# Windowed attention and a mixture of experts: expert 0's second weights and the zero blocks issued later, nine value slots, and gate logits in pieces of 64 keys by 32 columns

## The chip, the cores and the metric

The kernel runs on one core of a Trainium2 chip. The metric is the device time of one execution in microseconds (us). Matmuls run on TensorE (PE; the loading of their weights is shown apart, as PEld), elementwise work on VectorE (DVE), ScalarE (ACT) and GpSimd (POOL). SyncE (SP) issues most of the DMA transfers, in the order in which they are written.

## The reference

Attention over a window of 64 positions, then a layer of 8 experts of which each row takes its best two.

```python
scores = scale * np.matmul(q, k.transpose(0, 1, 3, 2))      # 8 batches, 8 heads, 576 positions, 64 dims
mask = (rel >= 0) & (rel < window)                           # window = 64
attn = softmax(np.where(mask, scores, -1e9))
x = np.matmul(attn, v) ...                                   # rows of 512: N = 4608
noisy_logits = x @ w_gate + np.log1p(np.exp(x @ w_noise)) * noise
top2 = the two largest of 8 per row, with softmax weights
for e in range(E):                                           # E = 8, w1 512 x 1024, w2 1024 x 512
    h = np.maximum(x[mask] @ w1[e], 0.0)
    out[mask] += top2_w[mask, k, None] * (h @ w2[e])
```

## The kernel before

The attention is done in 36 units. A unit j is a block of 64 positions (i = j // 4) of a pair of batches (bp = j % 4), with all 8 heads. The loop over j, near the end of the program, is a software pipeline written out by hand: in iteration j PE does the scores of unit j (`scores`), the product with the values of unit j-2 (`pv`), the transposes of the probabilities of unit j-1 (`transp`) and the gate logits of the values of unit j (`logits`). ACT copies the scores out of PSUM (`soft_a`, tile t), takes the exponential (`soft_b`, tile p), scales the output of unit j-3 (`norm_b`, tile x) and copies the logits out (`logits_copy`). DVE puts in the previous block's scores (`soft_max`), takes the maximum, masks the transposed probabilities (`apply_mask`, tile pt) and does most of the routing. POOL subtracts the maximum (line 342) and builds one-hot rows for the routing (line 592). Each engine runs its instructions in the order written.

The gate logits are linear in the attention output. So the gate's weights are multiplied with the values first: each value slot VW holds, beside four groups of values, a fifth group of 16 columns with the logits of each key, and `pv` averages them over the window together with the values. `logits` makes them on PE from a transposed copy of the values (vT, tile vt): for each of four pairs q of heads one matmul with 128 keys as weight columns (two batches of 64) and 64 moving columns, of which each key needs 32. `logits_copy` therefore takes for each half of the partitions the half of the columns that belongs to it, in two instructions.

Loads go through SP: q and k three units ahead, values (`load_v`, line 131) behind `pv`, vT (`load_vt`, line 137) behind `logits`. A value slot is a half of a tile VW[bp], for an even or an odd block: the load for unit j+2, issued behind `pv(j-2)`, overwrites values that this very `pv` reads. vT has two buffers, and the load for j+2 overwrites the one that `logits(j)` reads.

Two more kinds of transfer stand in that loop. In units 32 to 35 the second weights of expert 0 are loaded (`load_w2`, line 219; 8 pieces of 256 KB). They go to the tile ws, and `split_w2` (lines 243 and 235) cuts them into two parts while the first layer of expert 0 runs. From unit ZFROM = 36 on, `zero_out` (line 199) writes blocks of 128 rows of zeros to the output, three a unit, 38 blocks in all; the rest of them is spread over the layers of expert 0. The experts' results are added to the output by indirect transfers from POOL (line 966), which need the zeros of their rows first.

Units 36 to 38 only finish the pipeline. Between their pieces, and before that from unit 32 on the transposes for it (line 734), the first layer of expert 0 (`up(0, 0)`) begins. What follows is the work on the experts, 16 pairs of layers, in which PE runs almost without a gap.

Of the kernel before, what the change touches and what calls it, by code (L numbers as in the profile page):

```python
# [8 lines left out]
F32 = mybir.dt.float32  # L9
# [4 lines left out]
AF = mybir.ActivationFunctionType  # L14
# [6 lines left out]
NP = B // 2  # L21
NT = NP * NB
# [21 lines left out]
SLOTS = 5  # L44
WARM = 4

ZFROM = 36
PACED = 12
HOLD = 4
RATE = ((16, 8), (99, 7))  # L50
# [38 lines left out]
def tile_kernel(ctx, tc, qT, kT, vx, vT, wgx, noise, w1, w2, out):  # L89
    nc = tc.nc  # L90
# [14 lines left out]
    acon = at.enter_context(tc.tile_pool(name="acon", bufs=1))  # L105
    ld = at.enter_context(tc.tile_pool(name="ld", bufs=2))
    wk = at.enter_context(tc.tile_pool(name="wk", bufs=2))
# [1 line left out]

    KW = acon.tile([128, NP, 2, H, 64], F32)  # L110

    VW = [acon.tile([128, 2, 5, 2, 4, 17], F32, name=f"vw{j}") for j in range(NP)]
    QC, VT = {}, {}

    def load_q(j):
# [12 lines left out]

    def load_v(j):
        i, bp = divmod(j, NP)  # L130
        nc.sync.dma_start(VW[bp][:, i % 2, 0:4], vx[bp, i])


    def load_vt(j):
        i, bp = divmod(j, NP)
        VT[j] = ld.tile([128, 4, 128], F32, name="vt", bufs=2)
        nc.sync.dma_start(VT[j], vT[bp, i])

    for j in range(2):
# [33 lines left out]
    nc.vector.tensor_scalar(mcur, mprev, -1.0, 1.0, op0=OP.mult, op1=OP.add)  # L173

    maskT = acon.tile([128, 2, 2, 64], F32)
    other = acon.tile([128, 2, 64], F32)
    o3 = ones.rearrange("p (u r) -> p u r", u=2)
    nc.gpsimd.affine_select(maskT[:, 0], o3, pattern=[[0, 2], [1, 64]], base=0, channel_multiplier=-1,
                            compare_op=OP.is_ge, fill=0.0)
# [2 lines left out]
    nc.vector.tensor_copy(maskT[64:128, 0], other[64:128])  # L182
    nc.vector.tensor_scalar(maskT[:, 1], maskT[:, 0], -1.0, 1.0, op0=OP.mult, op1=OP.add)
    for v in VW:
        nc.gpsimd.memset(v[:, :, 4], 0.0)


    noise_sb = consts.tile([128, NT, E], F32)
# [28 lines left out]
    def load_w2(e, ks=slice(0, KF)):  # L217
        if e < E:
            nc.sync.dma_start(w2s[:, ks], w2[e][:, ks])
# [57 lines left out]
        return lag([(w2s[:, f], W2["h"][:, f], W2["l"][:, f]) for f in (0, 4, 1, 5, 2, 6, 3, 7)])  # L277


    VG = idle[:, 0:256].rearrange("p (n c) -> p n c", n=1)  # L280

    def logits(j):
        p = VG[:, 0]
        x = VT.pop(j)
        for u in range(2):
            for g in range(2):
                q = u * 2 + g
                nc.tensor.matmul(p[:, q * 64:q * 64 + 64], lhsT=x[:, q, :], rhs=wgx_sb[:, g], start=True, stop=True)

    def logits_copy(j):  # L290
        i, bp = divmod(j, NP)
        for a in range(2):
            h = slice(a * 64, a * 64 + 64)
            nc.scalar.activation(VW[bp][h, i % 2, 4, :, :, 0:16].rearrange("p u (g x) e -> p (u g) x e", x=2),
                                 VG[h, 0].rearrange("p (k a x e) -> p k a x e", a=2, x=2, e=16)[:, :, a], AF.Copy)

    ST, T, P, TP, PT, XT = {}, {}, {}, {}, {}, {}

# [67 lines left out]
    def pv(j):  # L366
        i, bp = divmod(j, NP)
        o = aps.tile([128, 2, 512], F32, name="ps_o", bufs=2)
        OT[j] = o
        PO[j] = o[:, :, 0:340].rearrange("p a (k d) -> p a k d", d=85)  # L370
        pt, v = PT.pop(j), VW[bp]
        for g in range(2):
            for x in range(2):
                for w in range(2 if i else 1):
                    for a in range(2):
                        for u in range(2):
                            pa = slice(a * 64, a * 64 + 64)
                            nc.tensor.matmul(PO[j][u * 64:u * 64 + 64, a, g * 2 + x, :],  # L378
                                             lhsT=pt[pa, w, u * 2 + g, x * 64:x * 64 + 64],
                                             rhs=v[pa, (i + w) % 2, :, u, g * 2 + x, :],  # L380
                                             start=(w == 0), stop=(w == 1 or not i))
        if j + NP < NT:
            load_v(j + NP)
# [64 lines left out]
    for k in (1, 2, 4, 8, 16, 32):  # L448
        n = min(k, NT - k)
# [654 lines left out]
    for j in range(NT + 3):  # L1104
        if j == TURN:
            for q, f in enumerate(turn(0, 0)):
                aux.setdefault(j + q // 2, []).append(f)

        if 0 < j < PACED:
            load_k(j + 3)  # L1110
        on(store, j - 4)
        blanks(j)
        if j < 2:
            load_v(j + 2)
        if NT - 4 <= j < NT:
            load_w2(0, slice((j - NT + 4) * 2, (j - NT + 4) * 2 + 1))
        on(norm_a, j - 3)
        drain(rate(0))
        on(scores, j)
        if j < NT - 3:  # L1120
            load_q(j + 3)
        if W1G // 2 - 4 <= j < W1G // 2 + 4:
            k = j - W1G // 2 + 4
            load_w1(0, slice(k // 2, k // 2 + 1), slice(k % 2 * F // 2, (k % 2 + 1) * F // 2))
        if 2 < j < 3 + len(REST):
            REST[j - 3]()
        on(soft_a, j)
        on(soft_b, j - 1)
        ahead(2)
        drain(rate(1))  # L1130
        on(pv, j - 2)
        on(place_slots, j - 2)
        if PACED <= j < NT - 3:
            load_k(j + 3)
        if NT - 4 <= j < NT:
            load_w2(0, slice((j - NT + 4) * 2 + 1, (j - NT + 5) * 2))
        blanks(j)
        on(norm_b, j - 3, 0)
        on(soft_max, j)
        on(soft_max2, j)  # L1140
        if placed:
            add_slots(placed.pop())
        drain_slots(1)
        if j < NP:
            warm(WARM)
        on(transp, j - 1)
        ahead(2)
        on(logits, j)
        if j < NT - 2:
            load_vt(j + 2)  # L1150
        blanks(j)
        on(norm_b, j - 3, 1)
        on(apply_mask, j - 1)
        drain(rate(2))
        on(logits_copy, j)
        ahead(2)
        on(gate, j - 3)
        drain(rate(3))
        drain_slots(2 if j >= DENSE else 1 + j % 2)
        for f in aux.get(j, ()):  # L1160
            f()
        drain(rate(4))
# [18 lines left out]
    for n, (e, c) in enumerate(work):  # L1181
        nxt = work[n + 1] if n + 1 < len(work) else None
        last = c == len(chunks(e)) - 1
        side, parts = [], []
        if n == 2:
            load_counts()
        if n == 0:
            halves = split_w2()
            side += halves[:5]
            parts.append((0.0, 1.0, [lambda: drain_slots(1)] * 9))  # L1190
            parts.append((0.0, 0.35, [zero_out] * 7))

            def catch_up():
                while (0, 1, 2) not in XG:
                    drain(1)
                    drain_slots(1)
        elif n == 1:
            pending.append(count())
            parts.append((0.0, 0.9, [lambda: (drain(1), drain_slots(1))] * 18))
            parts.append((0.0, 0.9, [zero_out] * 8))  # L1200
            side += [settle, lambda: drain_slots(10 ** 6), lambda: [x() for x in first_list(2)]]
        elif c == 0:
            parts.append((0.55, 1.0, split_w2()))
        if nxt and n:
            rows_of = gather(*nxt)
            if n < 2:
                side += [lambda: None] * 2 + rows_of
            else:
                parts.append((0.0, 0.65, rows_of))
        if last and nxt:  # L1210
            nextw = split_w1(e == 0)
            parts += ([(0.55, 0.75, nextw[0]), (0.8, 1.0, nextw[1])] if e else
                      [(a, b, nextw[q]) for q, a, b in ((0, 0.02, 0.12), (1, 0.14, 0.3), (2, 0.33, 0.5), (4, 0.34, 0.5),
                                                       (3, 0.55, 0.75), (5, 0.56, 0.75), (6, 0.8, 1.0))])
        parts.append((0.92 if n == 1 else 0.0, 1.0, side))
        spread(up(e, c) if n else up00, 52 if e else KF * KD - (0 if n else len(taken)), *parts)
        side = turn(*nxt) if nxt else []
        total = KF * len(tiles(e, c)) + (4 if e else 0) - (KF - 1 if chunks(e)[c] % 128 else 0)
        free = 12.5 / total
        if e == 0:  # L1220
            parts = [((0.66, 0.98) if n == 0 else (0.5, 0.97) if n == 1 else (0.02, 0.7)) + (side,)]
            if last:
                parts.append((0.7, 0.98, nextw[7]))
        else:
            if c == 0:
                load_w1(e + 1)
            parts = [(free, 0.86, side)]
            if last and nxt:
                parts.append((free, 0.9, nextw[2] + nextw[3]))
        if n == 1:  # L1230
            load_w1(1)
            parts.append((0.0, 0.6, list(other_lists())))
            parts.append((0.0, 0.4, [zero_out] * len(blank)))
        if n == 0:
            parts.append((0.0, 0.16, halves[5:]))
            parts.append((0.1, 0.96, [lambda: drain(2)] * 24))
            parts.append((0.0, 0.9, [zero_out] * 13))
            parts.append((0.0, 0.6, [lambda: drain_slots(1)] * 6))
            parts.append((0.64, 0.65, [catch_up]))
        spread(down(e, c), total, *parts)  # L1240
        if last:
            load_w2(e + 1)
# [118 lines left out]
```

## Time and profile before

| what | value |
|---|---|
| median of 3 runs | 998.04 us (997.68 to 999.22) |
| the profiled execution | 997.35 us |
| its span, first to last instruction | 995.3 us |
| mean granted TensorE clock | 0.997 of full speed |
| PE busy | 956.3 us (96% of the span) |
| DVE / ACT / POOL busy | 689.9 / 525.9 / 320.1 us |

The share of PE is a mean over a long part in which it is full and a first part of about 195 us in which it is not. Times below are counted from the first instruction of the profiled execution.

### The profile page before, as it was taken

The page shows a single profiled execution, that of the slowest core. Times are in us where ns is not written, and L with a number is a line of the kernel's source. Part 1 is how long each engine was busy: PE and PEld are TensorE (multiplying, and loading weights), DVE is VectorE, ACT ScalarE, POOL GpSimd, SP SyncE. Part 2 cuts the span into 40 slices and gives each one's busy share as a digit, 9 for nine tenths or more (in the row PEclk, how much of TensorE's full clock was granted, in tenths as well). Part 3 has the DMA queues.
Part 4 walks back from the last instruction along what each step waited for, and adds up shares of the span by engine and source line. Part 5 has one row for each costly group of instructions (what it writes and reads, how often), then busy time and mean ns, then how long its engine had stood idle before and what let it go on. Part 6 is the DMA issues. An engine that isn't in the chain of part 4 may idle for free. (4 is left out here: it accounts for less than half of the span.)

```text
span 995.3 us, 21900 instructions
## 1 busy us (share of the span) xinstructions
PE 956.3 (96%) x8408; PEld 858.2 (86%) x8408; DVE 689.9 (69%) x1728; ACT 525.9 (53%) x1346; POOL 320.1 (32%) x442
## 2 busy tenths in 40 slices
PE   8788888999999999999999999999999999999996
PEld 8777787888879888989898989898989898989895
DVE  5688898763786777767766786668666867686730
ACT  4888877522455545544554455445544554455531
POOL 5346546122322414040414141413131323241303
PEclk9999999999999999999999999999999999999999
DMA  9989997894649456854584458454945494647304
GB/s 326 365 270 314 287 294 273 271 263 119 153 89 267 81 130 132 252 73 120 116 265 70 125 115 267 60 134 87 283 63 143 73 266 89 149 93 206 48 1 56
DMA packets 107810, 168.93 MB, mean 170 GB/s; under 512 B 13424, under 2 KB 57712, under 8 KB 105904
## 3 DMA queue, kind: packets, MB, share of 16 engines
q1 hardware_dynamic: 90544, 126.96, 41.7%
q0 software_dynamic: 17152, 40.48, 21.9%
q8 instruction: 68, 1.11, 0.5%
q14 instruction: 46, 0.38, 0.1%
HBM read 110.08 MB, written 57.32 MB: 168 GB/s over the span
## 5 line engine op out<-in xcount | busy, mean ns | idle before, releaser
L966 POOL DMA_INDIRECT out_dram<-xg,los x70 | 111.9, 1598 | 427.5 <-ACT xh L774 124.3
L900 ACT ACTIVATE hb<-tq 128x288 fp32r<-128x288 f32 (+1 forms) x168 | 76.9, 458 | 143.9 <-DVE tq L919 143.7
L1038 PE MATMUL ps_d<-w2h,hb 128*128 128x512 f32 x392 | 152.9, 390 | 0.0
L1039 PE MATMUL ps_d<-w2l,hb 128*128 128x512 f32 x392 | 152.8, 390 | 0.0
L1040 PE MATMUL ps_d<-w2h,hb 128*128 128x512 f32 x392 | 152.7, 390 | 0.0
L919 DVE TENSOR_TENSOR tq<-ps_z,tq 128x288 f32<-128x288 f32 (+1 forms) x168 | 79.2, 472 | 89.0 <-PE ps_z L890 88.5
L888 PE MATMUL ps_z<-xh,WH 128*128 128x288 f32 (+1 forms) x448 | 137.5, 307 | 0.9
L889 PE MATMUL ps_z<-xl,WH 128*128 128x288 f32 (+1 forms) x448 | 135.2, 302 | 0.0
L890 PE MATMUL ps_z<-xh,WL 128*128 128x288 f32 (+1 forms) x448 | 135.2, 302 | 0.0
L904 DVE SCALAR_TENSOR_TENSOR hb<-tq,hb 128x320 fp32r<-128x320 f32 (+2 forms) x168 | 75.6, 451 | 37.5 <-ACT hb L900 35.2
L888 PEld LDWEIGHTS ps_z<-xh,WH 128*128 128x128 f32 x448 | 84.0, 188 | 5.5 <-DVE tq L919 3.7
L1040 PEld LDWEIGHTS ps_d<-w2h,hb 128*128 128x128 f32 x392 | 73.6, 188 | 15.6
L1038 PEld LDWEIGHTS ps_d<-w2h,hb 128*128 128x128 f32 x392 | 73.6, 188 | 14.0
L1039 PEld LDWEIGHTS ps_d<-w2l,hb 128*128 128x128 f32 x392 | 73.6, 188 | 13.8
L889 PEld LDWEIGHTS ps_z<-xl,WH 128*128 128x128 f32 x448 | 84.1, 188 | 1.1
L890 PEld LDWEIGHTS ps_z<-xh,WL 128*128 128x128 f32 x448 | 84.1, 188 | 0.0
L698 POOL DMA_INDIRECT xg<-xrows,lxs x70 | 69.0, 986 | 23.2 <-issue 22.6
L782 ACT ACTIVATE xh<-tq 128x512 fp32r<-128x512 f32 (+1 forms) x70 | 42.7, 610 | 61.9 <-DVE tq L778 60.5
L235 DVE TENSOR_TENSOR WL<-ws,WH 128x512 fp32r<-128x512 f32 x112 | 67.2, 615 | 6.6 <-ACT WH L243 6.5
L399 ACT ACTIVATE x<-ps_o,r 128x80 f32<-128x80 f32 x288 | 67.0, 350 | 7.5 <-DVE r L389 7.2
L378 PE MATMUL ps_o<-vw,pt 64*64 64x85 f32 x2176 | 49.9, 235 | 12.7 <-issue 8.2
L342 POOL TENSOR_TENSOR t<-t,mx 128x512 f32<-128x512 f32 x36 | 38.8, 1078 | 70.8 <-DVE mx L341 49.2
(242 smaller groups left out, 2347.0 us busy)
## 6 DMA issues: line engine op xcount, KB each, us to landing
ws<-in_w_dram SPq DMA_DIRECT2D x14, 2048.0 KB, 11.5
xs<-xg SPq DMA_DIRECT2D x63, 256.0 KB, 3.4
vw<-in_vx_dram SPq DMA_DIRECT2D x36, 272.0 KB, 4.5
out_dram<-zero SPq DMA_DIRECT2D x38, 256.0 KB, 4.6
qc<-in_qT_dram SPq DMA_DIRECT2D x36, 256.0 KB, 4.8
KW<-in_kT_dram SPq DMA_DIRECT2D x36, 256.0 KB, 4.9
vt<-in_vT_dram SPq DMA_DIRECT2D x36, 256.0 KB, 4.6
xrows<-x SPq DMA_DIRECT2D x36, 256.0 KB, 4.9
```

Source lines behind the costliest of these rows:

```text
L235: eng.tensor_tensor(l, x, h.bitcast(F32), op=OP.subtract)
L698: nc.gpsimd.indirect_dma_start(out=XG[e, c, q][:m], out_offset=None, in_=X[:DUMP + seen.get((e, c), NT) * 128], in_offset=bass.IndirectOff ...
L888: nc.tensor.matmul(p[:, :n], lhsT=WH[:, a, k, w], rhs=xh[:, b, k, :n], start=first and k == 0, stop=False, **free)
L889: nc.tensor.matmul(p[:, :n], lhsT=WH[:, a, k, w], rhs=xl[:, b, k, :n], start=False, stop=False, **free)
L890: nc.tensor.matmul(p[:, :n], lhsT=WL[:, a, k, w], rhs=xh[:, b, k, :n], start=False, stop=(k == 1), **free)
L900: nc.scalar.activation(hh[:, f, a:b], src, AF.Relu)
L904: nc.vector.scalar_tensor_tensor(hl[:, f, a:m], src[:, :m - a], 0.0, hh[:, f, a:m].bitcast(F32), op0=OP.max, op1=OP.subtract)
L919: nc.vector.tensor_tensor(t, a[:, :n], t, op=OP.add)
L966: s = nc.gpsimd.indirect_dma_start(out=out[:(2 + seen.get((e, c), NT)) * 128], out_offset=bass.IndirectOffsetOnAxis(ap=LT[e, c][1][q][:m], ...
L1038: nc.tensor.matmul(p, lhsT=h, rhs=w2h[:, f, :], **a)
L1039: nc.tensor.matmul(p, lhsT=h, rhs=w2l[:, f, :], start=False, stop=False)
L1040: nc.tensor.matmul(p, lhsT=l, rhs=w2h[:, f, :], **b)
```

## The change

Four edits. The value slots become nine tiles, used in turn by j, and vT gets a third buffer. The logits are made with 64 keys and 32 columns in a matmul, so that each half of the partitions gets only its own columns; one copy then takes them all. The second weights of expert 0 are loaded in units 34 to 37. No zero block is written in units 36 to 38 any more, and the first layer of expert 0 issues 16 instead of 7. A mask's scratch tile moves to another pool, to make room.

```diff
-ZFROM = 36
+ZFROM = NT + 3
...
-    VW = [acon.tile([128, 2, 5, 2, 4, 17], F32, name=f"vw{j}") for j in range(NP)]
+    VW = [acon.tile([128, 5, 2, 4, 17], F32, name=f"vw{j}") for j in range(2 * NP + 1)]
...
-        nc.sync.dma_start(VW[bp][:, i % 2, 0:4], vx[bp, i])
+        nc.sync.dma_start(VW[j % len(VW)][:, 0:4], vx[bp, i])
...
-        VT[j] = ld.tile([128, 4, 128], F32, name="vt", bufs=2)
+        VT[j] = ld.tile([128, 4, 128], F32, name="vt", bufs=3)
...
-    other = acon.tile([128, 2, 64], F32)
+    other = wk.tile([128, 8, 64], F32, name="t")[:, 0:2]
...
-        nc.gpsimd.memset(v[:, :, 4], 0.0)
+        nc.gpsimd.memset(v[:, 4], 0.0)
...
-                nc.tensor.matmul(p[:, q * 64:q * 64 + 64], lhsT=x[:, q, :], rhs=wgx_sb[:, g], start=True, stop=True)
+                for a in range(2):
+                    h = slice(a * 64, a * 64 + 64)
+                    nc.tensor.matmul(p[h, q * 32:q * 32 + 32], lhsT=x[:, q, h], rhs=wgx_sb[:, g, a * 32:a * 32 + 32],
+                                     start=True, stop=True)
...
-        for a in range(2):
-            h = slice(a * 64, a * 64 + 64)
-            nc.scalar.activation(VW[bp][h, i % 2, 4, :, :, 0:16].rearrange("p u (g x) e -> p (u g) x e", x=2),
-                                 VG[h, 0].rearrange("p (k a x e) -> p k a x e", a=2, x=2, e=16)[:, :, a], AF.Copy)
+        nc.scalar.activation(VW[j % len(VW)][:, 4, :, :, 0:16].rearrange("p u (g x) e -> p (u g) x e", x=2),
+                             VG[:, 0].rearrange("p (k x e) -> p k x e", x=2, e=16), AF.Copy)
...
-        pt, v = PT.pop(j), VW[bp]
+        pt, v = PT.pop(j), [VW[(j - w * NP) % len(VW)] for w in range(2)]
...
-        if NT - 4 <= j < NT:
-            load_w2(0, slice((j - NT + 4) * 2, (j - NT + 4) * 2 + 1))
+        if NT - 2 <= j < NT + 2:
+            load_w2(0, slice((j - NT + 2) * 2, (j - NT + 2) * 2 + 1))
...
-            parts.append((0.0, 0.35, [zero_out] * 7))
+            parts.append((0.05, 0.75, [zero_out] * 16))
```

On PE, a unit of the middle of the attention (scores, values, transposes, logits, and the next unit's scores), before:

```order
L318 MATMUL ps_s<-KW,qc 64x128 x16
L378 MATMUL ps_o<-vw_91,pt 64x85 x32
L354 MATMUL ps_t<-ident,p 128x128 x4
L288 MATMUL ps_g<-wgx_sb,vt 128x64 x4
L318 MATMUL ps_s<-KW,qc 64x128 x16
```

The end of that unit and the start of the next one, now:

```order
L379 MATMUL ps_o<-vw_98,pt 64x85 x4
L355 MATMUL ps_t<-ident,p 128x128 x4
L290 MATMUL ps_g<-wgx_sb,vt 64x32 x8
L319 MATMUL ps_s<-KW,qc 64x128 x16
L379 MATMUL ps_o<-vw_94,pt 64x85 x4
L379 MATMUL ps_o<-vw_90,pt 64x85 x4
```

The four logits matmuls have become eight of a smaller shape in the same place; the product with the values reads two tiles in turn.

On SP, a unit's loads in the middle of the attention with the semaphores that each waits for (DMAHW: an earlier transfer of SP's own; PE, Activation: an engine), before:

```order
L402 DMA xrows<-x 128x512 [waits DMAHW0_49,Activation_49]
L118 DMA qc<-in_qT_dram 128x512 [waits DMAHW1_49,PE_49]
L131 DMA vw_92<-in_vx_dram 128x544 [waits DMAHW2_49,PE_49]
L122 DMA KW<-in_kT_dram 128x512 [waits DMAHW3_49]
L137 DMA vt<-in_vT_dram 128x512 [waits DMAHW4_49,PE_49]
```

And now:

```order
L403 DMA xrows<-x 128x512 [waits DMAHW0_49,Activation_49]
L118 DMA qc<-in_qT_dram 128x512 [waits DMAHW1_49,PE_49]
L131 DMA vw_93<-in_vx_dram 128x544 [waits DMAHW2_49]
L122 DMA KW<-in_kT_dram 128x512 [waits DMAHW3_49]
L137 DMA vt<-in_vT_dram 128x512 [waits DMAHW4_49]
```

The loads of values and vT no longer wait for PE. On SP at the end of the attention (L402 and L403 are the stores of the attention's rows, L579 and L580 of the gate weights, L199 the zero blocks), before:

```order
L219 DMA ws<-in_w_dram 128x512 x2
L579 DMA xrows<-xc 128x6x16
L402 DMA xrows<-x 128x512
L199 DMA out_dram<-zero 256x1x256 x3
L402 DMA xrows<-x 128x512
L199 DMA out_dram<-zero 256x1x256 x3
L402 DMA xrows<-x 128x512
L199 DMA out_dram<-zero 256x1x256 x3
L402 DMA xrows<-x 128x512
L199 DMA out_dram<-zero 256x1x256 x19
L579 DMA xrows<-xc 128x9x16
```

And now:

```order
L580 DMA xrows<-xc 128x6x16
L403 DMA xrows<-x 128x512
L219 DMA ws<-in_w_dram 128x512 x2
L403 DMA xrows<-x 128x512
L219 DMA ws<-in_w_dram 128x512 x2
L403 DMA xrows<-x 128x512 x2
L199 DMA out_dram<-zero 256x1x256 x28
L580 DMA xrows<-xc 128x9x16
```

The last two pairs of w2 pieces stand where six zero blocks stood, and all zero blocks up to the last gate weights stand in one row.

## Rows read from the trace of the kernel before

**Rows 1.** Stretches, columns: PE, PEld, DVE, ACT, POOL busy (x), clock, DMA share, GB/s.

```profile
20.28:48.53 28.25, 22.38 (x586) 20.66 (x585) 17.94 (x28) 22.88 (x84) 10.52 (x12) 0.98 1.02 366
53.46:149.79 96.33, 83.25 (x2323) 75.36 (x2322) 86.55 (x217) 79.68 (x304) 52.39 (x60) 1.00 0.92 293
...
194.88:995.30 800.42, 788.72 (x4402) 704.71 (x4401) 536.27 (x1351) 382.89 (x819) 224.11 (x306) 1.00 0.58 138
```

**Rows 2.** Timeline of PE, a clean unit: start, us, what [idle before, releaser].

```profile
24.10 1.10 PE L318 MATMUL ps_s<-KW,qc 64*64 64x128 f32 x32
...
26.50 0.66 PE L354 MATMUL ps_t<-ident,p 128*128 128x128 f32 x4 [0.71 <-ACT p L346]
27.00 1.00 PE L288 MATMUL ps_g<-wgx_sb,vt 128*128 128x64 f32 x8
27.93 1.10 PE L318 MATMUL ps_s<-KW,qc 64*64 64x128 f32 x32
```

**Rows 3.** Timeline of ACT, the same unit.

```profile
25.34 0.60 ACT L328 ACTIVATE t<-ps_s 128x512 f32<-128x512 f32 x1 [0.36 <-PE ps_s L318]
...
28.04 0.56 ACT L294 ACTIVATE vw<-ps_g 64x128 f32<-64x128 f32 x2
...
29.16 0.60 ACT L328 ACTIVATE t<-ps_s 128x512 f32<-128x512 f32 x1 [0.36 <-PE ps_s L318]
```

**Rows 4.** Timeline of PE's weight loads: scores of 64 columns, and logits.

```profile
13.06 0.56 PEld L320 LDWEIGHTS ps_s<-KW,qc 64*64 64x64 f32 x32
...
26.89 0.97 PEld L288 LDWEIGHTS ps_g<-wgx_sb,vt 128*128 128x128 f32 x8
```

**Rows 5.** Waits of DVE, 53.46 to 149.79: us in total, times, longest.

```profile
DVE r L389 <- ACT r L388: 1.9, 3, 0.8
DVE t L336 <- ACT t L328: 1.6, 4, 0.5
...
DVE pt L359 <- PE ps_t L354: 0.7, 1, 0.7
```

**Rows 6.** Waits of the SP queue, 50 to 150 us.

```profile
SPq L137 <- PE ps_g L288: 14.6, 19, 2.0
SPq L131 <- PE ps_o L378: 11.7, 12, 1.9
```

**Rows 7.** Tile vt: its DMA.

```profile
DMA to landing us min/median/max: 3.7/4.6/6.6
```

**Rows 8.** Waits of PE, 0 to 195 us.

```profile
PE ps_o L378 <- issue: 8.2, 9, 2.9
```

**Rows 9.** Timeline of PE, units 32 to 34.

```profile
153.19 0.80 PE L378 MATMUL ps_o<-vw,pt 64*64 64x85 f32 x26 [1.57 <-issue]
...
161.70 0.66 PE L734 MATMUL ps_t<-ident,xg 128*128 128x128 f32 x4 [1.24 <-DVE pt L359]
```

**Rows 10.** Timeline of POOL, the start: blanking the value slots.

```profile
2.24 1.11 POOL L185 MEMSET vw<- 128x272 f32 x4
```

**Rows 11.** Timeline of DVE, the first unit.

```profile
8.35 0.72 DVE L336 COPY_PREDICATED t<-mcur,ps_s 128x512 f32<-128x512 uint32 x1 [4.05 <-POOL t L330]
```

**Rows 12.** Timeline of the SP queue, from unit 36 on.

```profile
178.34 0.57 SPq L402 DMA_DIRECT2D xrows<-x  x1
...
187.18 16.29 SPq L199 DMA_DIRECT2D out_dram<-zero  x19
...
211.19 0.38 SPq L579 DMA_DIRECT2D xrows<-xc  x1
```

**Rows 13.** Timeline of POOL, the first add into the output and the next gather.

```profile
202.66 1.67 POOL L966 DMA_INDIRECT out_dram<-xg,lo  x1 [5.65 <-ACT xg L999]
...
232.82 1.02 POOL L698 DMA_INDIRECT xg<-xrows,lx  x1 [15.12 <-PE ps_z L847]
```

**Rows 14.** Timeline of ACT, the last splits of w2.

```profile
195.46 1.66 ACT L243 ACTIVATE w2h<-ws 128x512 fp32r<-128x512 f32 x3
```

**Rows 15.** DMA issues: KB each, median us to landing.

```profile
ws<-in_w_dram SPq DMA_DIRECT2D x16, 256.0 KB, 5.1
```

More of the change, by code (lines that the diff above doesn't have):

```diff
@@ L277, in split_w2 @@
         return lag([(w2s[:, f], W2["h"][:, f], W2["l"][:, f]) for f in (0, 4, 1, 5, 2, 6, 3, 7)])
-    VG = idle[:, 0:256].rearrange("p (n c) -> p n c", n=1)
+    VG = idle[:, 0:128].rearrange("p (n c) -> p n c", n=1)
     def logits(j):
@@ L379, in pv @@
                                              lhsT=pt[pa, w, u * 2 + g, x * 64:x * 64 + 64],
-                                             rhs=v[pa, (i + w) % 2, :, u, g * 2 + x, :],
+                                             rhs=v[w][pa, :, u, g * 2 + x, :],
                                              start=(w == 0), stop=(w == 1 or not i))
@@ L1134, in tile_kernel @@
             load_k(j + 3)
-        if NT - 4 <= j < NT:
-            load_w2(0, slice((j - NT + 4) * 2 + 1, (j - NT + 5) * 2))
+        if NT - 2 <= j < NT + 2:
+            load_w2(0, slice((j - NT + 2) * 2 + 1, (j - NT + 3) * 2))
         blanks(j)
```

## The prediction

> **What bounds the kernel now.** I read the table by stretches first. Its last line, from 194.88 us on, has PE busy 788.72 of 800.42 us: there only the number of matmuls counts, and the change adds or removes none of them. So a gain can only come from the 195 us before, and it passes to the end one for one, since everything behind it follows in order. The lines of that part [rows 1], each cut where a unit's scores begin on PE, tell two things. In 20.28 to 48.53 the DMA share is 1.02, against 0.92 in the stretch after it. In 53.46 to 149.79, the 21 units 11 to 31, DVE is busy 86.55 of 96.33 us, PE 83.25 and ACT 79.68: three engines close to their limit, DVE the closest.
>
> Then the timeline of PE and ACT for a unit without routing work. Scores to scores on PE is 27.93 - 24.10 = 3.83 us [rows 2]. The loop is: scores, the copy and the exponential on ACT, then the transposes, which start 2.40 us after the scores and waited 0.71 us for the exponential (p); then 0.50 us to the logits, then 0.93 us of logits until the next scores. **The eight logits passes stand inside the loop.** ACT idles 0.36 us a unit for the scores, and its two value copies start at 28.04, 1.12 us before its next copy of scores [rows 3]. So here PE's loop leads and ACT is 0.36 us behind it.
>
> The waits of the SP queue come next: from 50 to 150 it stood 14.6 us behind the logits (L137, the next vT) and 11.7 us behind PV (L131, the next values) [rows 6]. But vT is issued two units before its use, some 9 us by the mean unit of 96.33 / 21 = 4.59, and lands after at most 6.6 us [rows 7]. Values, q and k are issued further ahead. The waits of SP are real, and no row shows an engine that pays for them.
>
> **The logits, on PE.** Now 4 matmuls a unit with 128 columns of weights and 64 of keys, in two passes each: 8 loads in 0.97 us [rows 4], 117 ns from one to the next (0.93 / 8). After: 8 matmuls, 16 passes, each with half the weight columns and half the moving columns. No row has such a shape. Lower bound: 32 loads of 64 x 64 with 64 columns take 0.56 us [rows 4], 17.5 ns each; 16 of them would be 0.28 us. Upper bound for a gain: half a load of 117 ns, 58 ns, times 16 gives 0.93 us and nothing is won. The 64 x 64 passes run four abreast, 70 ns a round of four. The new shape can run two abreast, so 8 rounds of 70 ns: I take 0.56 us, a gain of 0.37 us a unit in the loop.
>
> [...]
>
> **The value copies, on ACT.** Two copies of 64 partitions become one of 128 with the same 128 elements. The pair takes 0.56 us [rows 3], so ACT is freed of 0.28 us a unit. In a clean unit that stays behind PE's loop: ACT's 3.46 us of work become 3.18, PE's loop 3.83 - 0.37 = 3.46.
>
> **What that is worth, by stretch.** Units 4 to 7 are clean, so up to 4 x 0.37 = 1.5 us; units 8 to 10 also split weights on ACT, 3 x 0.28 = 0.8 us. Against the 2.3 us stands the DMA share of 1.02: bytes do not become fewer. Both ends are open; I take half, 1.1. In units 11 to 31 DVE sets the ceiling: 96.33 - 86.55 = 9.8 us of idle time, and below it nothing. The part of it that ended with ACT's reciprocal input, ACT's copy of scores or PE's transposes, which is where a shorter loop would show, is 1.9 + 1.6 + 0.7 = 4.2 us [rows 5]. I take 3.5, since DVE's waits elsewhere grow when PE and ACT run ahead. In units 32 to 35 the logits end before DVE has freed the transposes' bank, and PE waits there up to 1.24 us [rows 9]: shorter logits only lengthen that wait, so nothing.
>
> **Second weights two units later.** Units 32 and 33, which still load k, q, values and vT, lose four pieces of w2. In that traffic PE stood still 1.57 us in the middle of PV with no signal named [rows 9]. Such stops are 8.2 us in 9 places before 195 us [rows 8]; they fall where DMA is loaded, and the cause is not shown. I take half, 0.8 us. The late side is covered: the last pair goes out behind the store of 178.34 [rows 12], and a piece lands in 5.1 us [rows 15], so about 185, while the last three splits of w2 start at 195.46 [rows 14]. If that cover went, PE would wait for w2 in the second layer.
>
> **Zero blocks.** Nine leave units 36 to 38, so the first layer's queue holds 28 in one row instead of 19. These cost 16.29 us for 19 [rows 12], 0.86 each. The first add into the output needs 16 of them. They would be issued by 187.18 + 16 x 0.86 = 200.9 and have landed about 5 us later, at 206, while the add ran at 202.66 [rows 13]: 3 us late. Behind it on POOL come two more adds and then a gather that waited 15.12 us for PE anyway [rows 13], so it is hidden. The row of 28 ends at 187.2 + 24 = 211.3, where SP waited for the last gate weights already, until 211.19 [rows 12].
>
> **Nine value slots, three vT buffers.** No time from the SP waits, as said. One cost: POOL blanks 9 slots instead of 4 of twice the size. Four took 1.11 us [rows 10], 0.28 each; nine take between 1.25 (half of it each) and 2.5. I take 0.19 each, 1.7 us: 0.6 us later. All POOL work up to the first unit's fill is back to back, and DVE waited 4.05 us for that fill [rows 11], so the 0.6 goes to the end in full.
>
> **Sum.** -1.1 - 3.5 - 0.8 + 0.6 = -4.8 us. The profiled execution took 997.35 us (span 995.3 and 2.05 around it), which gives 992.55. The median of the runs is 998.04, 0.69 above the profiled one, so 993.2.
>
> **Rivals.** The bound that this measurement can tell from no change is 0.2%, 2 us.
> (a) Nothing to see: the half-wide loads run one after another at 58 ns and the logits stay near 0.93 us, or DVE holds the middle whatever PE does. Then of the 3.5 us about 1 is left, from the value copies, and of the 1.1 about 0.3: with the 0.8 and the 0.6 it is -1.5, 996.5. For it: DVE's 90%. Against: the 4.2 us in which DVE itself waits for ACT and PE. [...]
> (b) Slower: 16 passes in the new mode cost over 58 ns each. At 80 ns the logits take 1.28 us, 0.35 more, inside the loop of 36 units; with half of the units bound there that is +6, 1004. It decides from 58 ns on. For it: a third array shape each unit and 8 more matmuls, each with its load, through PE's queue. Against: the 17.5 ns.
> (c) More: PE's stops go with the calmer SP queue and most of DVE's idle time is won: -(2.3 + 7 of the 9.8 + 1.6 + 1 of the other stops) + 0.6 = -11, 987.
> (d) The wider reach of SP floods the DMA rings early, and PE's stops grow by as much as is won: 998, within the bound.
>
> **Chances.** Forecast, 991 to 996: 0.60. (c): 0.10. (a) and (d) together: 0.18. (b): 0.12. Faster by over 0.2%: 0.70; within: 0.18; slower: 0.12. The range goes from 988.5, leaving the better half of (c) out, to 998.8, which takes in most of (a) and (d) and leaves out (b).
>
> **What would show it.** In the profile after: the 16 logits passes in about 0.56 us, and the next scores that long after them; one value copy of 0.27 us; the clean units near 3.5 us apart; SP's waits at L131 and L137 gone; POOL's blanking about 1.7 us; DVE's share in units 11 to 31 above 0.90; the stop near 152 us gone; the first add some 3 us behind its eviction. I am wrong if the logits take over 0.93 us, if the units in the middle stay 4.59 us apart on the mean, or if w2's splits wait for DMA.

## The result: 0.9% slower, and the profile after

| | before | after |
|---|---|---|
| median of 5 runs beside each other, us | 998.04 (997.68 to 1000.4) | 1007.35 (1004.1 to 1008.1) |
| profiled execution, us | 997.35 | 1004.1 |
| its span, us; mean granted clock | 995.3; 0.997 | 1002.4; 0.990 |
| start of the first down matmul, us | 194.88 | 201.99 |
| its span behind that start, us | 800.42 | 800.41 |
| PE's stops with no signal named, 0 to 205 us | 9.2 us in 10 | 18.4 us in 19 |

The ratio is 1.0089, with an interval of 1.0068 to 1.011: slower, where 0.9952 was forecast, and outside the range. Behind the first down matmul nothing changed, so the profiled loss of 6.75 us (7.11 in the span, with 0.36 us less around it) is that of the stretch before. The starts of units place it: up to unit 4 the changed kernel is 0.21 us ahead, from unit 4 to 11 it gains 0.52, in units 11 to 31 it loses 6.22 (102.55 against 96.33 us), in units 32 to 34 another 1.73 (20.12 against 18.39), and behind them it gains 0.11: 7.11 in all.

The table by stretches, columns and places as in [rows 1] (the third line is units 32 to 35 and a little more):

```profile
20.07:47.55 27.48, 22.42 (x637) 19.48 (x633) 16.74 (x28) 20.24 (x77) 9.88 (x13) 0.94 1.01 354
52.73:155.28 102.55, 83.04 (x2494) 70.79 (x2490) 87.59 (x217) 73.24 (x285) 54.32 (x61) 0.97 0.87 284
155.28:181.00 25.72, 19.80 (x514) 17.04 (x514) 20.62 (x54) 15.40 (x55) 14.81 (x18) 0.93 0.52 172
```

In the middle no engine has much more work (POOL 1.9 us, DVE 1.0), PE's loads are busy 4.6 us less and ACT 6.4 us less, and DVE's share falls from 0.90 to 0.85. The last columns are new: the granted clock is 0.94, 0.97 and 0.93, where [rows 1] has 0.98 and 1.00 for the first two (up to unit 11 as a whole it is 0.95 in both kernels), and in the middle the DMA share fell.

The loop itself did what was forecast. PE in a clean unit, against [rows 2]:

```profile
69.39 1.10 PE L319 MATMUL ps_s<-KW,qc 64*64 64x128 f32 x32
...
71.79 0.66 PE L355 MATMUL ps_t<-ident,p 128*128 128x128 f32 x4
72.38 0.66 PE L290 MATMUL ps_g<-wgx_sb,vt 128*64 128x32 f32 x16
72.97 0.45 PE L319 MATMUL ps_s<-KW,qc 64*64 64x128 f32 x8
```

From the logits to the next scores it is 72.97 - 72.38 = 0.59 us (0.93 before), scores to scores 3.58 us (3.83 before); the transposes start 2.40 us after the scores, as before. From transposes to logits it is 0.59 instead of 0.50 us. So the loop is 0.25 us shorter wherever it runs undisturbed. What disturbs it is in the waits of PE, 0 to 202 us (us in total, times, longest), against [rows 8]:

```profile
PE ps_o L379 <- issue: 8.8, 9, 1.7
PE ps_s L319 <- issue: 5.9, 6, 1.7
...
PE ps_g L290 <- issue: 2.9, 3, 1.6
PE ps_t L355 <- ACT p L347: 2.7, 5, 0.7
...
PE ps_t L355 <- issue: 0.8, 1, 0.8
```

"Issue" is time in which PE waited for nothing that the profile shows. Within units 11 to 31 alone these stops went from 3.3 us to 11.3 (6.2, 3.0, 1.3 and 0.8), 8.0 us more, against the 6.2 that the stretch lost. Three in a row, in the timeline of PE:

```profile
153.21 0.96 PE L379 MATMUL ps_o<-vw,pt 64*64 64x85 f32 x38 [1.70 <-issue]
...
158.34 0.80 PE L379 MATMUL ps_o<-vw,pt 64*64 64x85 f32 x28 [1.23 <-issue]
...
165.03 0.66 PE L379 MATMUL ps_o<-vw,pt 64*64 64x85 f32 x21 [1.42 <-issue]
```

They fall in the middle of PV, where no signal is waited for, with 38, 28 and 21 of its 64 passes left. Counted between them: 38 of PV, 4 transposes, 16 logits, 32 scores and 36 of the next PV are 126 passes, each with a load, so 252 instructions; between the second and the third it is 127 passes. The page's part on DMA queues has a queue for instructions:

```profile
q8 instruction: 71, 1.16, 0.5%
```

71 packets of 1.16 MB are 16 KB each; before there were 68. The page counts 8,696 passes of PE and as many loads, 17,392 in all, which is 67.9 times 256; before it is 16,816, 65.7 times. So an estimate, from the number of the packets and the distance of the stops, is that a packet holds 256 of PE's instructions; what is in a packet the profile does not tell. The traces hold the times of these packets, and they stand right beside the stops:

| | the 16 KB packet, us | PE's stop, us | from the packet's end to PE's next pass, us |
|---|---|---|---|
| before | 150.80 to 151.68 | 151.62 to 153.19 | 1.51 |
| after | 151.02 to 151.99 | 151.51 to 153.21 | 1.22 |
| after | 156.10 to 157.12 | 157.11 to 158.34 | 1.22 |
| after | 162.68 to 163.64 | 163.61 to 165.03 | 1.39 |

Counted over all of PE's records (passes, loads and the semaphore instructions between them, which make up the rest to 256), 162 of the 230 stops in the sixteen profiles of this case lie at the same place in a row of 256, record 193 or 194, whatever the kernel, though a unit has 108 passes before and 116 now. Each of the 162 ends 1.0 to 1.7 us (1.4 in the median) after such a packet has ended. The reading taken from these places and times is that PE has run through a block of 256 instructions before the next one has arrived. These stops are 7.5 us in 7 places before and 16.7 us in 16 now. The other 68, 37 of 186 us in all, lie elsewhere, many at the same place of the program in several kernels. The longest of them before is 0.94 us and ends at 138.19, 0.1 us after DVE has written pt (136.87 + 1.22): a wait for DVE that the view does not name.

A second loss follows some of the times in which PE stands still. Per us, columns as in [rows 1]:

```profile
145.00:146.00 1.00, 0.00 (x0) 0.00 (x0) 0.97 (x5) 1.00 (x6) 0.42 (x1) 1.00 0.91 261
146.00:147.00 1.00, 0.86 (x37) 0.86 (x40) 0.60 (x1) 1.00 (x6) 0.24 (x1) 0.82 0.97 250
147.00:148.00 1.00, 1.00 (x22) 0.81 (x17) 0.00 (x0) 0.30 (x3) 0.85 (x2) 0.50 1.13 315
148.00:149.00 1.00, 1.00 (x10) 0.67 (x10) 0.21 (x1) 0.00 (x0) 0.91 (x1) 0.50 0.89 275
149.00:150.00 1.00, 1.00 (x22) 0.94 (x24) 1.00 (x2) 0.21 (x2) 0.00 (x0) 0.50 0.90 340
150.00:151.00 1.00, 1.00 (x47) 1.00 (x43) 0.86 (x5) 0.72 (x5) 0.00 (x0) 0.97 0.90 328
```

PE did nothing for the whole of the first us (the stop of 1.55 us before 146.14), and from 146.6 to 150.1 it was granted 0.50 of full speed. Such dips come four times before 195 us here, once before the change. Three of the four begin behind a stop at a block's end (1.61, 1.55 and 1.42 us). The fourth, from 64.7 us, begins behind two waits with a signal (0.62 us for DVE and 0.79 for ACT), and one of the four in e1 (below) behind a wait of 1.48 us for DVE, so late instructions are not the only thing that goes ahead of a dip.

DVE, in 52.73 to 155.28, against [rows 5]:

```profile
DVE pt L360 <- PE ps_t L355: 5.8, 5, 2.2
DVE t L337 <- ACT t L329: 2.9, 6, 0.7
DVE r L390 <- ACT r L389: 1.3, 2, 0.7
```

Its wait for PE's transposes went from 0.7 to 5.8 us: DVE is late because PE is.

SP's waits at the logits and at PV [rows 6] are gone. In their place, 0 to 190 us:

```profile
SPq L118 <- PE ps_s L319: 22.6, 20, 3.5
SPq L403 <- ACT vw L295: 14.6, 5, 6.7
```

SP now waits once a unit, for the scores to free q's buffer, and then issues q, values, k and vT together; the stores of rows wait for ACT (the second line). The head of the kernel and the zero blocks, in the timeline of POOL, against [rows 10] and [rows 13]:

```profile
2.23 1.42 POOL L185 MEMSET vw<- 128x136 f32 x9
...
212.92 1.67 POOL L967 DMA_INDIRECT out_dram<-xg,lo  x1 [8.99 <-DMA out_dram<-zero]
...
239.94 1.02 POOL L699 DMA_INDIRECT xg<-xrows,lx  x1 [15.13 <-PE ps_z L848]
```

### The profile page after: what moved, and what is told of

It is laid out like the page before. It is cut to its first block, busy times and chain, and to the rows that moved or that the text cites. A ratio compares the mean times of both kernels' runs of the same rounds, so it can differ in the third digit from the quotient of the medians.

```text
span 1002.4 us, 22388 instructions
## 1 busy us (share of the span) xinstructions
PE 955.0 (95%) x8696; PEld 849.4 (85%) x8696; DVE 691.4 (69%) x1728; ACT 514.1 (51%) x1310; POOL 324.3 (32%) x447
## 3 DMA queue, kind: packets, MB, share of 16 engines
q8 instruction: 71, 1.16, 0.5%
## 5 line engine op out<-in xcount | busy, mean ns | idle before, releaser
L379 PE MATMUL ps_o<-vw,pt 64*64 64x85 f32 x2176 | 52.5, 241 | 12.8 <-issue 8.8
```

## The experiments

The theory formed from this profile: the narrow logits let PE run through its instructions faster (232 a unit instead of 216, in a shorter loop), so it outruns their supply more often, and after some stops the clock falls (B in the expectations). Its rival: the nine slots, whose loads now go out in a burst. Later B was split: B1 says that the number of instructions alone decides, D that the clock falls because the narrow logits leave PE less busy.

"Stops" below are PE's "issue" time from 0 to 205 us in the one profiled execution; "clock" is the mean granted clock over all timed runs of the kernel (before: 0.9956 over 28 runs beside the first four experiments, 0.9944 beside e5 to e8, 0.9959 beside e9 to e12, 0.9961 beside e13 and e14); medians are given with before's beside the same runs. How far the stops of one kernel differ from execution to execution was not measured.

**Each part by itself (e1 to e4).** Edits of the diff, applied alone: the narrow logits with the single copy; the slots with three vT buffers; the later w2 and zero blocks; and all but the slots.

```diff
# e1
+ for a in range(2):
+     h = slice(a * 64, a * 64 + 64)
+     nc.tensor.matmul(p[h, q * 32:q * 32 + 32], lhsT=x[:, q, h], ...)
# e2
+ VW = [acon.tile([128, 5, 2, 4, 17], F32, name=f"vw{j}") for j in range(2 * NP + 1)]
+ VT[j] = ld.tile([128, 4, 128], F32, name="vt", bufs=3)
# e3
+ ZFROM = NT + 3
+ if NT - 2 <= j < NT + 2:
+     load_w2(...)
# e4: e1 and e3
```

> The kernel before with the narrow logits and the single copy alone. Theory A (the burst of loads behind the scores, which the nine slots allow, holds up PE's stream of instructions): 993 to 996 us, stops of PE with no signal named before the first layer stay near the 9 us of before. Theory B (16 more PE instructions a unit and fewer busy columns bring the stops and the lower clock): 1003 or more, stops near 18 us.

> The kernel before with the nine value slots and three vT buffers alone. Theory A: 1001 to 1006 us, stops of PE well above 9 us, SP's loads in one burst behind the scores. Theory B: within 1.5 us of before, stops near 9 us.

> The kernel before with the second weights two units later and the zero blocks in the first layer alone. Theories A and B alike: 996 to 998 us (at most the 1.57 us stop near 152 us is won). A third theory, C (the later zero blocks or the later second weights hold up the first layers): 1002 or more, with the loss behind unit 35.

> The changed kernel without the nine slots and the third vT buffer: narrow logits, second weights and zero blocks as changed, old value slots. Theory A: 992 to 996 us. Theory B: 1003 or more, as the changed kernel.

| | ratio to before | median (before 997.70) | stops, us | clock |
|---|---|---|---|---|
| e1, logits | 1.0065 [1.0045, 1.0084] | 1003.21 | 19.3 in 22 | 0.9903 |
| e2, slots | 1.0028 [1.0008, 1.0048] | 1000.49 | 10.0 in 12 | 0.9937 |
| e3, late | 0.9991 [0.9971, 1.0011] | 995.98 | 8.1 in 10 | 0.9952 |
| e4, logits and late | 1.0079 [1.0053, 1.0106] | 1005.25 | 20.0 in 19 | 0.9887 |

The logits alone bring most of the loss, with after's stops and its clock. The three parts add up to 6.5 + 2.8 - 0.9 = 8.4 thousandths, against 8.9 for all; e4 has 7.9 where its two parts give 5.6, within the intervals. Waits of PE in e1, 0 to 205 us:

```profile
PE ps_o L379 <- issue: 7.9, 9, 2.2
PE ps_s L319 <- issue: 6.1, 8, 1.9
PE ps_g L290 <- issue: 3.6, 3, 1.9
```

They are after's lines without any change on SP, so the burst is not needed for the stops. The slots cost 2.8 us with stops about as before: the stops are theory B's, the time lies between what A and B expected. Of this 0.3 us is seen (unit 4's scores at 20.61 instead of 20.28), and the clock is 0.002 lower.

**Number or pace (e5, e6).** e5 is the kernel before with four one-column matmuls behind the wide logits, 8 passes with 8 loads: also 232 instructions a unit, in a longer unit. e6 is e1 with 4 of the 32 matmuls of PV left out: 216 instructions, in e1's short unit.

```diff
# e5
+ for q in range(4):
+     nc.tensor.matmul(idle[0:64, 340 + q:341 + q], lhsT=ones[0:64, 0:64], rhs=ones[0:64, 0:1], ...)
# e6
- for w in range(2 if i else 1):
+ n = 2 if i and g + x < 2 else 1
+ for w in range(n):
...
- start=(w == 0), stop=(w == 1 or not i))
+ start=(w == 0), stop=(w == n - 1))
```

> The kernel before with four matmuls of one column behind each unit's logits, their results unused: 8 passes and 8 weight loads more on PE, as many as the narrow logits add, shapes and copies as before. Theory B1 (the number of PE instructions: each 256 of them come in one 16 KB transfer, and more of them a unit are late more often): stops of PE before the first layer from 9 us to 15 or more, 1002 us or more. Theory B2 (not the number but the narrow shape, which keeps less of PE busy or runs through its instructions faster): stops stay near 9 us, and the time rises only by the eight passes, at most 0.25 us a unit in the clean units, to 998 to 1001.

> Narrow logits and the single copy, as in the run of these alone, with 4 of the 32 value matmuls of a unit left out (the previous block's part for one of four head pairs, so the output lacks it): PE has as many instructions a unit as before. Theory B1: stops back near 9 us, 990 to 995 us. Theory B2: stops stay near 20 us, 1000 us or more.

e5: 1.0031 [1.0009, 1.0054], 1002.59 against 999.02, clock 0.9967; a clean unit takes 4.29 us. Its waits of PE, 0 to 205 us:

```profile
PE ps_o L380 <- issue: 4.2, 6, 1.0
...
PE ps_g L288 <- issue: 1.2, 1, 1.2
...
PE ps_s L320 <- issue: 0.5, 2, 0.2
```

That is 5.9 us: as many instructions as after has, and fewer stops than before. B1 falls. The time is over what B2 expected, since the eight passes took 0.47 us a unit and not at most 0.25. e6: 0.9975 [0.9956, 0.9995], 996.39, stops 12.0 in 14, clock 0.9932, a clean unit of 3.57 us; time and stops lie between what B1 and B2 expected. What orders the stops is the pace, instructions of a unit by the length of a clean unit (e8 and e12, below, have before's pace):

| | instructions / clean unit, us | a us | stops, us | of them at a block's end, us |
|---|---|---|---|---|
| e5 | 232 / 4.29 | 54 | 5.9 | 5.0 |
| before (e2, e3, e8, e12) | 216 / 3.82 | 57 | 9.2 (10.0, 8.1, 11.9, 9.8) | 7.5 (7.4, 6.3, 9.4, 5.5) |
| e6 | 216 / 3.57 | 61 | 12.0 | 10.6 |
| after, e1, e4 | 232 / 3.57 | 65 | 18.4, 19.3, 20.0 | 16.7, 17.5, 17.9 |

The five kernels at before's pace spread from 8.1 to 11.9 us, so e6 stands clear of them at block ends alone; what tells pace from number is e5.

**Lighter DMA (e7, e13, e14).** If the stops are late instructions, they must shrink when other transfers get out of their way. vT is loaded for the first two units only (256 KB a unit less), in e1, in the kernel before, and in after.

```diff
-        VT[j] = ld.tile([128, 4, 128], F32, name="vt", bufs=2)
-        nc.sync.dma_start(VT[j], vT[bp, i])
+        if j < 2:
+            VTS.append(ld.tile([128, 4, 128], F32, name="vt", bufs=2))
+            nc.sync.dma_start(VTS[j], vT[bp, i])
+        VT[j] = VTS[j % 2]
```

> Narrow logits and the single copy, with the transposed values loaded for the first two units alone and used again by the others (the gate logits are then wrong): a fifth of the loads of a unit is gone, the engines' work is the same. If the stops are instructions that arrive late behind SP's loads (B1, and B2 by pace): stops fall under 9 us and the time to 988 to 995. If they have nothing to do with DMA: stops stay near 20 us, 1001 or more.

> The kernel before (wide logits, two copies) with the transposed values loaded for the first two units alone (gate logits wrong), as in the run of narrow logits with light DMA. If the narrow logits do shorten PE's loop and lose it again to late instructions, they must win where the instructions come in time: then this kernel is slower than the narrow one with light DMA (ratio 0.9988 to before), and its own stops are 0 to 4 us. But its 9 us of stops go too, so by sum: 998 - 5 = 993, ratio 0.993 to 0.997, and the narrow logits win nothing even there. If the stops of before do not depend on DMA: 997 to 999, stops near 9 us.

> The changed kernel whole, with the transposed values loaded for the first two units alone (gate logits wrong). If its loss is instructions that come late behind the loads: stops from 18 us to 5 to 9 us, and 996 to 1000 us (ratio 0.998 to 1.002 to before). If the loss is in the slots or in the shape: 1004 or more.

e7: 0.9988 [0.9969, 1.0007], 996.83 against 999.02, clock 0.992. Waits of PE in e7, 0 to 205 us:

```profile
PE ps_o L382 <- issue: 4.1, 7, 1.2
...
PE ps_s L322 <- issue: 2.7, 3, 1.6
PE ps_g L293 <- issue: 2.1, 1, 2.1
```

e13: 0.9962 [0.9945, 0.9978], 995.39 against 999.30, stops 5.7 in 10, clock 0.9968. e14: 0.9990 [0.9971, 1.0008], 999.21, clock 0.9942. Waits of PE in e14, 0 to 205 us:

```profile
PE ps_o L382 <- issue: 8.6, 12, 2.2
...
PE ps_s L322 <- issue: 2.3, 4, 0.7
...
PE ps_g L566 <- issue: 0.9, 1, 0.9
...
PE ps_g L293 <- issue: 0.2, 1, 0.2
```

With the same instructions the stops fall from 19.3 to 8.9 us (e7), from 9.2 to 5.7 (e13) and from 18.4 to 12.0 (e14); at block ends from 17.5 to 7.1, from 7.5 to 2.7 and from 16.7 to 8.3. So they hang on what else DMA carries. The 16 KB packet itself takes about 1.0 us in all six, but it starts earlier: from PE's entry into a block to the start of the next block's packet it is 2.6 us in the median and 2.0 with the lighter load (e1, e7), 2.5 and 2.0 (before, e13), 2.8 and 2.2 (after, e14), between 20 and 150 us. And there is never a block in store: at every block's end up to 185 us, with a stop or without, these six traces have just the packet ended that PE needs next, and not the one after it. The stops of e13 and e14 are above what was expected (0 to 4 and 5 to 9 us), and e7's time is above the 988 to 995. In this traffic the change costs 2.8 thousandths (0.9990 - 0.9962, with intervals that just overlap) instead of 8.9. But the narrow logits still win nothing: e7 is not below e13, though those ran beside different runs of before.

**The clock (e9, e10, e11).** A filler matmul (128 x 128 weights, 72 columns) in each unit keeps PE busier. It stands ahead of the transposes, where PE waits anyway, in e9 (the late part, wide logits) and e10 (e4); in e11 (e1) it stands behind the logits, in the loop.

```diff
+    def fill(n):
+        for _ in range(n):
+            nc.tensor.matmul(idle[:, 328:400], lhsT=ones, rhs=ones[:, :72], start=True, stop=True)
```

> The run with second weights and zero blocks moved alone, and in units 4 to 35 one matmul more ahead of the transposes, where PE waits for the exponential (128 x 128 weights, 72 columns, result unused; two passes, some 0.23 us). Theory D (PE's clock falls to its lower level after a stop where the passes around it keep PE too little busy): mean clock over the runs from 0.995 to 0.997 or more, 993.5 to 995.5 us. Rival E (clock falls follow the stops alone, and the filler only adds instructions): mean clock 0.995 or less, 997 or more.

> Narrow logits, single copy, second weights and zero blocks moved (the run without the slots), with the same filler in PE's wait. Theory D: mean clock from 0.989 to 0.994 or more, 997 to 1001 us. Rival E: clock near 0.989, 1004 or more.

> Narrow logits and single copy alone, with the same filler behind the logits, where PE does not wait: the clean unit gets some 0.23 us longer again and PE's instructions come at about 236 in 3.8 us, 62 a us, between the 60 of the run with fewer value matmuls (stops 12 us) and the 65 of the narrow logits alone (21 us). Theory B2 by pace (a stop comes when PE eats a 16 KB block of instructions faster than the next one comes in): stops 12 to 17 us, 997 to 1001 us. Rival (the narrow shape itself brings the stops): 20 us or more, 1003 or more.

All three stand against a median of 999.87. e9: 1.0015 [0.9996, 1.0033], 1000.90, stops 8.6, clock 0.9964: no gain with wide logits, the time is rival E's, and the clock hardly moves (0.9952 in e3). e10: 1.0041 [1.0019, 1.0062], 1004.35, stops 15.9, clock 0.9937, where e4 has 1.0079, 20.0 and 0.9887: with narrow logits the kernel with more work on PE comes out faster, but the intervals overlap, and the time is above what D expected. e11: 1.0040 [1.0021, 1.0059], 1003.05, stops 10.6, clock 0.9940, where e1 has 1.0065 and 0.9903: even a filler that lengthens the loop loses nothing against e1; its stops are under the 12 to 17 us that were expected, its time above. D is borne out at most in part, by the clocks of the narrow logits; since the filler also slows the pace, it doesn't separate the clock from the stops.

**ACT's share and the burst (e8, e12).** e8 is before with one of the two value copies left out; e12 is e2 with vT in two buffers.

```diff
# e8
-        for a in range(2):
+        for a in range(1):
# e12
-        VT[j] = ld.tile([128, 4, 128], F32, name="vt", bufs=3)
+        VT[j] = ld.tile([128, 4, 128], F32, name="vt", bufs=2)
```

> The kernel before with one of the two copies of the logits left out (half of the gate logits stay zero): ACT alone is freed of 0.28 us a unit, PE as before. By the prediction's reading (PE's loop leads, ACT follows): 995.5 to 998. If ACT led: 988 to 994.

> Nine value slots alone, vT with two buffers as before: SP waits for the logits again, not for PV. If the burst of loads behind the scores costs the 2.8 us of the slots: about half of it comes back, 998 to 999.5 on the scale where before is 998. If the blanking of nine slots on POOL costs it: all of it stays, 1000 to 1001.

e8: 0.9978 [0.9956, 1.0000], 998.14 against 999.02, clean unit unchanged at 3.82 us, stops 11.9. ACT's relief alone is worth 1 us by the medians and 2 by the ratio, at the edge of what is told from nothing, and PE's loop leads. e12: 1.0019 [1.0002, 1.0037], 1002.29 against 999.87; stops 9.8, clock 0.9945. It overlaps e2, so it is not shown that what the slots cost hangs on vT's third buffer.

## Why the prediction was wrong

The step that failed is in the second-weights part and in rival (d): PE's stops with no signal named were taken as something that belongs to the DMA traffic of a place, of which half a stop, 0.8 us, could be won. They were not asked what a faster PE does to them. The row was there: a stop in the middle of PV with 26 passes left [rows 9], 8.2 us of such at PV [rows 8] (with one at the scores 9.2). The profile page's queue for instructions, and a count of PE's instructions between stops, would have led to it: that stop and six others of the ten are PE at the end of a block of 256 instructions, waiting for the next. Instead of -0.8 the stops brought +9.2 us (18.4 against 9.2, all of it at block ends, 16.7 against 7.5), more than the shorter loop can win. The sum also had no term for the clock.

- **The logits in the loop** were right: 0.59 us against 0.56, a clean unit of 3.58 against "near 3.5". It lies between the bounds of 0.28 and 0.93, and two abreast, which no row before had for this shape, was right: in the trace the loads start in pairs, 6 to 7 ns apart, with 58 ns from pair to pair (the prediction took 70), and the next scores start 0.19 us after the last pair. Why it is 0.09 us more from transposes to logits (0.59 against 0.50) is not shown.
- **-1.1 for units 4 to 10** measured -0.5 up to unit 11, with the DMA share at 1.00 before and 1.01 now and the clock at 0.95 in both kernels: of two open ends half was taken, and about half of that came, which says little about either.
- **-3.5 for units 11 to 31** measured +6.2. "DVE's waits elsewhere grow when PE and ACT run ahead" was the wrong limit: DVE waits more because PE is late, and its share falls instead of rising over 0.90.
- **-0.8 for the stop near 152 us** measured +1.7 in units 32 to 34: the w2 pieces left, and the narrow logits' stops came. Nor did that stop go where the late part stands alone: in e3 it is 1.26 us instead of 1.57. By itself the late part is the only one not slower, 0.9991 (e3), 1.7 us by medians, and the interval doesn't tell it from nothing.
- **Zero blocks and late w2** were right. The first add starts 212.92 - 201.99 = 10.93 us behind the first down matmul, 7.78 before: 3.15 us later, against 3. The gather behind it waited 15.13 us for PE as before, and the last splits of w2 stand 0.58 us behind the first down matmul in both profiles.
- **Blanking nine slots** took 1.42 us against 1.7, so +0.3 instead of +0.6: this term was sized too high. The slots cost more than that (e2, 2.8 us by medians), and where is open.
- **SP's waits** went, and no engine had paid for them: this was right.
- **Rival (b)** had the sign and not the cause: a pass costs 0.59 / 16 = 37 ns, under its 58, and the loop is shorter. **Rival (d)** had the mechanism of stops that eat what is won, but from SP's burst; e1 has the stops without a burst. It also let them grow only by as much as was won, and left out the clock.

How much each does: e1's mean clock is 0.0053 lower than before's. Over the runs of e1 and of before 0.001 less clock goes with 0.6 to 0.8 us more, so an estimate is 3.2 to 4.4 of e1's 5.5 us. The rest is stops less the loop's gain. This division is an estimate from a correlation, and it doesn't keep the two apart, since three of the four dips in the profile after begin behind a stop. That instruction blocks arrive late is shown by the packets beside the stops, by their place in every row of 256, and by what pace (e5) and DMA load (e7, e13, e14) do to them. Open also: what the other 68 stops are; why some stops are followed by the lower clock and others not (e11 has 10.6 us of stops up to 205 us, with no dip from 20 to 113 us and a mean granted clock of 0.997 in its profile; e7 has 8.9 and lost as much clock as after, the sum of 1 less the granted clock being 6.8 us in both), and whether a kernel that keeps the pace down elsewhere could keep the shorter loop. No version here is clearly faster than the kernel before with its work whole.

## What to carry to other kernels

Before splitting matmuls into smaller ones, count PE's instructions per us in the loop against stops "issue" in the profile: here they doubled from 9.2 us at 57 instructions a us to 18.4 at 65, with a DMA share of 0.90 and 0.82 from 20 to 195 us, and took more than the loop won. A stop in the middle of a row of matmuls with no signal named is worth a count of PE's instructions back to the last one; if it is always some 256 or a multiple, as for 162 of the 230 stops here, look for the instruction packet that ends before PE goes on (here 1.0 to 1.7 us before). Whether a shorter loop brings more of these stops is then the question to ask: here a clean unit of 3.57 us instead of 3.82 took them from 7.5 us to 16.7. And the granted clock by stretch is to be read beside them: from 20 to 195 us it was 0.99 before and 0.96 after.

## What was not expected of the hardware

- 162 of 230 stops of PE lie at the end of a block of 256 instructions (252 to 254 without the semaphore instructions) and end 1.0 to 1.7 us after a 16 KB packet of the instruction queue. The 230 last 0.15 to 3.0 us each; the DMA share from 20 to 195 us was 0.90 before, 0.82 after, and 0.72 in e14.
- After a stop of 1.55 us PE was granted 0.50 for about 3.4 us; four dips in a profile with 18.4 us of stops, none in e13 with 5.7 (granted 1.00 from 20 to 195 us).
- Passes of 128 x 64 weights with 32 columns come two abreast, 58 ns from pair to pair (37 ns a pass over the whole 0.59 us); eight passes of one column (64 x 64) took 0.47 us more in a unit (4.29 against 3.82), 59 ns each with their loads.
